# A retention layer with a feed-forward block: a fixed instruction order per engine in place of a software-pipelined loop

## Chip, cores, metric

One core of a Trainium2 chip. The metric is the time of one execution on the device in microseconds (us), the median of several runs. Engines are named as in the profile: PE (TensorE, matmuls), PEld (its weight loads), DVE (VectorE), ACT (ScalarE), POOL (GpSimd), SP (a queue that issues DMA transfers).

## The reference

Batch 4, 8 heads, 768 tokens, head size 64. First a retention recurrence per head; its output, with the heads side by side, is x (512 wide). Then a normalised feed-forward block with a residual:

```python
for t in range(S):
    state = gamma * state + einsum('bhd,bhe->bhde', k[t], v[t])
    y[t] = scale * einsum('bhd,bhde->bhe', q[t], state)
# x = y with the heads joined: [4, 768, 512]
xn = (x - mu) / sqrt(var + 1e-6) * g_ln
out = x + relu(xn @ w_ch1) @ w_ch2          # 512 -> 2048 -> 512
```

Both kernels work on tiles of 128 tokens: 24 tiles, 6 per batch entry, the recurrence in its chunked form (within a tile a masked 128x128 product, across tiles a state). Four tiles form a group, because the first product takes 512 tokens at once.

## The kernel before

One loop runs over the tiles. Each iteration has the work of several tiles in different stages: the first product runs six tiles behind the attention, the second nine behind. All inputs come as bf16 (converted in flight) on one DMA queue, which POOL issues, and one chunk of the weights follows each tile's q, k, v.

```python
for t in range(-2, NT + MM2_LAG):
    ...load_q(t+2); load_k(t+2); load_v(t+2)        # gpsimd queue, fp32 -> bf16
    ...vg = vsb * ks                                # DVE, later POOL
    # a quarter of the first product, tile t-6: four times
        for ko in range(KO): nc.tensor.matmul(pm1, w1[...], xnt[...])      # 512 wide
        nc.scalar.activation(out=h1[:, ho, :], in_=pm1, func=AF.Relu)
    # q and k of tile t+1 transposed into ptr (the one bank of tag "tp")
    # pa: 4 matmuls of one row half, then 4 of the other; two masks on DVE
    # second product of tile t-9: 16 matmuls, then the add and the store
    pxt = ptp.tile([P, H, P], BF16, tag="tp")       # xn of tile t-2, same bank as ptr
    for ko in range(KO): nc.tensor.transpose(pxt[:, ko, :], ...)
    for ko in range(KO): nc.scalar.mul(out=xnt[...], in_=pxt[:, ko, :], mul=gln[...])
    # py, pd of tile t-1
    nc.scalar.copy(out=x_all[:, ty, :], in_=py)     # ACT reads py
    ...ptmp = pd + pb_prev                          # DVE
    ...pb = ptmp * g128m                            # POOL
    nc.vector.bn_stats(out=stats, in_=py)           # DVE reads the same bank
    ...rstd, negms
    nc.scalar.activation(out=xn, in_=xg, func=AF.Identity, bias=negms, scale=rstd)
    # one chunk of w1 or w2 on the gpsimd queue
```

## Time and profile before

| | before |
|---|---|
| time, median of 3 runs (range) | 254.82 us (254.81 to 255.43) |
| span of the profiled run, PE busy | 253.1 us, 88% |
| first feed-forward product starts | 43.8 us (one matmul; the next at 44.6, which the prediction takes as the start) |
| one steady iteration | 9.06 us |
| last matmul ends | 249.0 us |

PE bounds this kernel once it has started, so its idle time is the table to read; the busy shares of the other engines (41 to 53%) bound nothing. The prediction below shows those lines. Two more come from the view of the waits (engine and line, what it waited for; microseconds in total, times, longest):

```profile
PE ptr L233 <- DMA qsb<-in_q_dram: 12.0, 7, 5.0
...
DVE stats L360 <- ACT x_all L334: 8.1, 18, 1.2
```

The first is the start, held up by q. The second looks harmless and was: DVE, which has plenty of idle time here, waits for ACT's copy before it may read the same PSUM bank.

### The profile page before, as it was taken

To read this page: it belongs to the slowest core of one execution; us is meant where nothing else is said; L and a number is where in the kernel's file an instruction comes from. 1 tells how busy PE (TensorE), PEld (TensorE's weight loads), DVE (VectorE), ACT (ScalarE), POOL (GpSimd) and SP (SyncE) were. 2 spreads that over 40 slices of the span, in tenths; PEclk is the share of its full clock that TensorE was granted. 3 is DMA by queue.
4 is the path that set the end of the run, shared out by engine and by line. 5 is a ranking of instruction groups with operands and counts; after the bars stand their busy time and mean duration, and the time that the engine had idled before them with its cause. 6 is when DMAs were issued, how large, how long until landed. Compare 5 with 4: busy or idle time off the path is not lost.

```text
span 253.1 us, 4043 instructions
## 1 busy us (share of the span) xinstructions
PE 222.4 (88%) x1577; PEld 118.0 (47%) x1600; DVE 104.5 (41%) x249; ACT 133.2 (53%) x295; POOL 109.7 (43%) x121
## 2 busy tenths in 40 slices
PE   0534666999999999999999999999999999999993
PEld 0323444555555545545554554555455444444441
DVE  5454476256364353535435434543544231111121
ACT  5133456699484476558447546744754475333100
POOL 8948589789985373337357530330110100000000
PEclk9999999999999999999999999999999999999999
DMA  6999999999999976494998550410110011111012
GB/s 42 119 182 183 186 176 175 172 88 108 95 125 105 62 85 80 65 65 62 93 68 91 71 40 39 62 44 0 44 41 19 25 43 41 41 44 41 12 71 83
DMA packets 83106, 20.18 MB, mean 80 GB/s; under 512 B 75920, under 2 KB 80016, under 8 KB 83088
## 3 DMA queue, kind: packets, MB, share of 16 engines
q0 software_dynamic: 79104, 13.64, 69.4%
q1 hardware_dynamic: 3984, 6.30, 6.6%
q8 instruction: 12, 0.20, 0.3%
q14 instruction: 6, 0.05, 0.0%
HBM read 27.27 MB, written 6.29 MB: 133 GB/s over the span
## 4 chain that ended last, share of the span: by engine, by line
PE 65%; ACT 14%; DMA 8%; DVE 5%; POOL 5%; issue 2%; POOLq 0%
PE pm L275 33%; PE pm L219 21%; DMA qsb<-in_q_dram 8%; ACT xntg L298 6%; DVE stats L360 3%; ACT h1g L226 3%; PE pa L250 2%; ACT x_all L334 2%; PE pxt L296 2%; PE ptr L233 2%; PE ptr L235 2%; ACT rstd L364 1%; POOL ksb L90 1%; POOL vsb L96 1%; ACT trs L240 1%
## 5 line engine op out<-in xcount | busy, mean ns | idle before, releaser
L219 PE MATMUL pm<-xntg,w 128*128 128x512 bf16 x364 | 88.6, 382 | 3.8 <-ACT h1g L226 1.6
L275 PE MATMUL pm<-w,h1g 128*128 128x512 bf16 x381 | 86.3, 380 | 0.2
L226 ACT ACTIVATE h1g<-pm 128x512 bf16<-128x512 f32 x96 | 55.5, 592 | 18.8 <-PE pm L219 14.6
L219 PEld LDWEIGHTS <-w 128*128 128x128 bf16 x384 | 36.7, 98 | 46.7 <-issue 9.9
L275 PEld LDWEIGHTS <-h1g 128*128 128x128 bf16 x384 | 36.3, 98 | 43.3
L298 ACT ACTIVATE xntg<-pxt,gln 128x128 bf16<-128x128 bf16 x96 | 27.4, 368 | 55.0 <-PE pxt L296 54.9
L283 DVE TENSOR_TENSOR osb<-pm,x_all 128x512 f32<-128x512 f32 x24 | 16.6, 692 | 76.9 <-PE pm L275 76.9
L257 DVE TENSOR_TENSOR asb<-pa,cm 128x512 bf16<-128x512 f32 x48 | 30.9, 683 | 7.7 <-PE pa L250 7.6
L203 POOL TENSOR_TENSOR vg<-vsb,ks 128x512 bf16<-128x512 bf16 x17 | 19.7, 1158 | 28.8 <-PE pd L342 19.2
L90 POOL DMA_DIRECT2D ksb<-in_k_dram x24 | 21.7, 906 | 20.2 <-PE pd L342 19.8
L355 POOL TENSOR_TENSOR pb<-ptmp,g128m 128x512 bf16<-128x512 bf16 x16 | 18.6, 1161 | 27.1 <-DVE ptmp L354 27.0
L237 DVE TENSOR_TENSOR trs<-ptr,qsT 128x512 bf16<-128x512 bf16 x24 | 10.2, 424 | 35.5 <-PE ptr L235 35.4
L84 POOL DMA_DIRECT2D qsb<-in_q_dram x24 | 21.9, 913 | 5.3 <-PE pa L250 2.2
L96 POOL DMA_DIRECT2D vsb<-in_v_dram x24 | 21.9, 916 | 3.6 <-POOL vg L203 1.8
L233 PE MATMUL ptr<-idn,qsb 128*128 128x128 bf16 x96 | 11.0, 245 | 12.0 <-DMA qsb<-in_q_dram 12.0
L376 ACT ACTIVATE xn<-x_all,negms,rstd 128x512 bf16<-128x512 bf16 x24 | 19.5, 811 | 3.1 <-DVE negms L367 2.4
L360 DVE BATCH_NORM_STATS2 stats<-py 128x6 f32<-128x512 f32 x24 | 16.7, 697 | 8.1 <-ACT x_all L334 8.1
L334 ACT CAST x_all<-py 128x512 bf16<-128x512 f32 x24 | 14.3, 597 | 9.4 <-PE py L326 5.7
L240 ACT COPY trs<-ptr 128x512 bf16<-128x512 bf16 x24 | 14.0, 585 | 6.5 <-DVE trs L237 6.5
L233 PEld LDWEIGHTS <-qsb 128*128 128x128 bf16 x96 | 7.6, 107 | 17.3 <-DMA qsb<-in_q_dram 13.3
L296 PE MATMUL pxt<-idn,xn 128*128 128x128 bf16 x96 | 10.1, 233 | 3.8 <-ACT trs L240 3.7
L250 PE MATMUL pa<-trs 64*128 64x128 bf16 x192 | 12.0, 243 | 1.6 <-ACT trs L240 1.6
(42 smaller groups left out, 137.1 us busy)
## 6 DMA issues: line engine op xcount, KB each, us to landing
out_dram<-osb SPq DMA_DIRECT2D x24, 256.0 KB, 2.0
w<-in_moe_w_ch_dram POOLq DMA_DIRECT2D x8, 512.0 KB, 9.0
qsb<-in_q_dram POOLq DMA_DIRECT2D x24, 128.0 KB, 4.5
ksb<-in_k_dram POOLq DMA_DIRECT2D x24, 128.0 KB, 4.4
vsb<-in_v_dram POOLq DMA_DIRECT2D x24, 128.0 KB, 4.2
gln<-in_moe_g_ln_dram SPq DMA_DIRECT2D x1, 2.0 KB, 2.2
```

The lines of the kernel that those rows point to most:

```text
L84: nc.gpsimd.dma_start(out=qsb, in_=qv[bl][cl])
L90: nc.gpsimd.dma_start(out=ksb, in_=kv[bl][cl])
L96: nc.gpsimd.dma_start(out=vsb, in_=vv[bl][cl])
L203: veng.tensor_tensor(out=vg, in0=vsb_of[ts_], in1=ks, op=ALU.mult)
L219: nc.tensor.matmul(pm1, lhsT=w1[:, ko, ho * P:(ho + 1) * P], rhs=xnt1[:, ko, :, :], start=(ko == 0), stop=(ko == KO - 1),)
L226: nc.scalar.activation(out=h1[:, ho, :], in_=pm1, func=AF.Relu)
L233: nc.tensor.transpose(ptr[:, pr, :], qsb[:, 2 * pr:2 * pr + 2, :], idn)
L257: nc.vector.tensor_tensor(out=asb[:, par_i], in0=pa, in1=cm4, op=ALU.mult,)
L275: nc.tensor.matmul(pm2, lhsT=h1[:, ho, q2 * P:(q2 + 1) * P], rhs=w2[:, ho, :], start=(ho == 0), stop=(ho == HO - 1),)
L298: nc.scalar.mul(out=xnt_of[tg][:, ko, ti, :], in_=pxt[:, ko, :], mul=gln[:, ko:ko + 1],)
L360: nc.vector.bn_stats(out=stats, in_=py.rearrange("p h d -> p (h d)"))
L376: nc.scalar.activation(out=xn, in_=xg, func=AF.Identity, bias=negms, scale=rstd)
```

## The change

The intent: start the dense part earlier (q and v take a second queue as fp32, weights are loaded between the token tiles), take work off ACT, DVE and POOL (g_ln goes into w1 once, the state is summed in PSUM), and write every engine's order by hand in place of a generic pipeline. The kernel declares its schedule manual: each engine's instructions keep the order in which they are written. The second product runs two groups behind the first. The core of the diff, with cuts:

```diff
-        qsb = qstg.tile([P, H, D], BF16, ...);  nc.gpsimd.dma_start(out=qsb, ...)
+        qsb[t] = qstg.tile([P, H, D], FP32, ...); nc.sync.dma_start(out=qsb[t], ...)
-    for t in range(-2, NT + MM2_LAG):
-        ... (above)
+    ctx.enter_context(tc.manual_schedule())
+    def scale_w1(j):                       # g_ln into a quarter of w1
+        for ko in range(KO):
+            nc.vector.tensor_scalar_mul(out=w1[:, ko, j*DM:(j+1)*DM], in0=..., scalar1=gln[:, ko:ko+1])
+    def att1(t, eng):   # ptr (tag "tp"): k and scaled q transposed; one copy of 1024 on ACT
+    def att2(t):        # pa: row halves in turn; one mask of 1024 on DVE
+    def att3(t):
+        # state part and tile part into py
+        nc.scalar.copy(out=x_all[:, t, :], in_=py)
+        nc.vector.bn_stats(out=stats, in_=py)
+        ...bn_aggr; sqrt on ACT
+        # pd: kept in PSUM, the next tile's matmuls add to it; pb = pd * mask on DVE
+        nc.vector.reciprocal(...)
+        nc.vector.tensor_scalar(out=xn[t], in0=x_all[:, t, :], scalar1=mv[:, 0:1], scalar2=rstd,
+                                op0=ALU.subtract, op1=ALU.mult)
+    def att4(t):        # pxt (tag "tp"): xn transposed; one copy of 512 on ACT
+    for t in range(GT):                    # the first four tiles, one after the other
+        scale_q(t, nc.gpsimd) ... scale_v(t, nc.vector)
+        att1(t); att4(t - 2) if t >= 2; att2(t); att3(t)
+    next_load(); next_load(); scale_w1(0)
+    att4(2); mm1(0, 0..1, tiles 0 to 2); att4(3); mm1(0, 0..1, tile 3)
+    def slot(a, g, quarter, m2, skip=0):
+        next_load()
+        scale_q(a, nc.gpsimd); scale_v(a, nc.gpsimd); att1(a)
+        # two chunks of the first product
+        if m2 is None and a - 1 in xn: att4(a - 1)
+        att2(a)
+        # two chunks of the first product
+        att3(a)
+        if m2 is not None:
+            mm2(m2)
+            att4(a)
+    for i in range(GT):
+        slot(4 + i, 0, i, None, skip=2 if i == 0 else 0)
+        if i < 3: scale_w1(i + 1)
+    att4(7)
+    for i in range(GT): slot(8 + i, 1, i, None)
+    att4(11)
+    for g in range(2, NG):                 # second product two groups later
+        for i in range(GT): slot(4*(g+1)+i or None, g, i, GT*(g-2)+i)
+    for t in range(GT*(NG-2), NT): mm2(t, tail=True)
```

## The prediction

> **What bounds the kernel now.** I read the page first: busy shares, then the slices.
>
> ```profile
> PE 222.4 (88%) x1577; PEld 118.0 (47%) x1600; DVE 104.5 (41%) x249; ACT 133.2 (53%) x295; POOL 109.7 (43%) x121
> ...
> PE   0534666999999999999999999999999999999993
> ...
> GB/s 42 119 182 183 186 176 175 172 88 108 95 125 105 62 85 80 65 65 62 93 68 91 71 40 39 62 44 0 44 41 19 25 43 41 41 44 41 12 71 83
> ```
>
> The row of PE has two parts. From the eighth slice on (44 us) TensorE is busy to the end; before that it works about half the time, and in just those slices the DMA engines move a level 180 GB/s. So there are two questions: how soon can the dense part start, and how much idle time is left in it. The chain of waits, in order of time, answers the first:
>
> ```profile
> 13.01 11.80 DMA qsb<-in_q_dram
> ...
> 32.48 7.60 DMA qsb<-in_q_dram
> ...
> 44.60 2.13 PE pm L219 x6
> ```
>
> The attention of the first seven tiles waits for q, which queues behind weights on the same full DMA queue. A tile of q, k, v and one weight chunk (0.92 MB as bf16) takes 0.92/180 = 5.1 us, and the first product (L219) starts only after seven such periods. For the second question I read TensorE's timeline over one steady iteration and near the end:
>
> ```profile
> 82.09 1.02 PE L219 MATMUL pm<-xntg,w 128*128 128x512 bf16 x4 [0.20 <-ACT h1g L226]
> 82.95 0.39 PE L233 MATMUL ptr<-idn,qsb 128*128 128x128 bf16 x4
> 83.18 0.39 PE L235 MATMUL ptr<-idn,ksb 128*128 128x128 bf16 x4
> 83.50 0.41 PE L250 MATMUL pa<-trs 64*128 64x128 bf16 x8
> 83.84 3.63 PE L275 MATMUL pm<-w,h1g 128*128 128x512 bf16 x16
> 87.30 0.39 PE L296 MATMUL pxt<-idn,xn 128*128 128x128 bf16 x4
> 87.52 0.40 PE L316 MATMUL py<-vg,asb 128*128 128x64 bf16 x8
> 87.76 0.39 PE L326 MATMUL py<-pb,trs 128*128 128x128 bf16 x4
> 87.98 0.39 PE L342 MATMUL pd<-vg,ksb 128*128 128x128 bf16 x4
> ...
> 209.99 0.39 PE L296 MATMUL pxt<-idn,xn 128*128 128x128 bf16 x4
> ...
> 210.83 1.89 PE L219 MATMUL pm<-xntg,w 128*128 128x512 bf16 x8 [0.46 <-ACT xntg L298]
> ```
>
> Differences of the starts give issue times: 16 second-product matmuls 3.46 us (216 ns each), four 128-wide ones 0.22 to 0.23, eight pa 0.34, eight py 0.23. A tile thus costs 2 x 3.45 for the two products and 0.45+0.34+0.23+0.22+0.22+0.23 = 1.69 for attention, 8.6 us. The iteration (82.95 to 92.01 for the next one's start) is 9.06, so some 0.4 us of it is stall. In all: 44.6 us of start; then 165.6 us of products and 28.4 of the remaining 17.7 tiles' attention (1.5 off for first and last chunks of a batch); the last matmul ends at 249.0. 249.0-44.6-194.0 = 10.4 us of stalls in the dense part. 4.1 us follow for the last add and store.
>
> The last two lines show a wait I need below: after a transpose into PSUM, a reader of ACT's copy of it is held. From 209.99, 0.39 for the matmuls, some 0.45 for one 128-wide ACT copy and the semaphores.
>
> **What the Trainium skill says.** "TensorE: Matmul & The Clock Gate", part 1: an array without sustained work runs at half rate. The trace agrees in its durations (four pxt at 27.44 took 0.58 us, later 0.39), though the granted clock reads 1.00 throughout. "VectorE: DVE Perf Modes", the TRN2 errata: an fp32 tensor-tensor takes (N+151)/0.96 ns, so one mask of 1024 elements is an estimated 1.22 us; the trace's 512-wide ones (about 690 ns) agree. "ScalarE: Activation LUTs", what ACT_TABLE_LOAD costs: 0.833 ns an element; from the 585 ns of the 512-wide L240 I estimate 585+427 = 1.01 us for one copy of 1024. "SBUF — State Buffer", who interferes with whom: a single-source DVE operation in a two-port mode and GpSimd lock each other out. No row of before shows it; the change brings such operations (xn, g into w1) beside two GpSimd multiplies per tile.
>
> **The change, part by part.**
>
> *Start.* q and v go to the SP queue and weights behind the first tiles, so data stops being the limit: 4 tiles at 2.5 us (q, k, v alone moved 155 to 160 GB/s around 45 us: 0.39 MB in 2.5) are there after some 12 us. What limits instead is the written order: att1, att2, att3 of one tile, then the next. At half clock I add up one tile: transposes 1.0, ACT copy 1.0, pa 0.62 (as at 14.30), mask 1.22, py with state 0.85, pd 0.43, and four hand-overs at 0.05: 5.3 us, 5.8 with a pxt between. With the first q scaled and transposed at about 5.5 us, four tiles end near 26.5. DVE then makes xn of tile 3 (about 2 us) before it can scale w1, so the first product starts near 28.5. Eight narrow products at a half-clock, att4(3) and its copy bring the first slot to 33 us. Before, at 44.6, had 2.3 more tiles of attention done (3.9 us), after has 1.7 us of product done: a lead of 44.6-33-2.2 = 9.4 us.
>
> *Slots 4 to 11 (no second product).* TensorE has 0.45+1.72+0.23+0.34+1.72+0.67 = 5.1 us a slot, ACT 4 relus at 0.51 issue time, copies of 0.92, 0.5, 0.5, and 0.25 for the root: 4.2 us. POOL has two multiplies at 1.16 and two issues at 0.9: 4.1. All fit. But scale_w1(i+1) is written after slot i, so on DVE it stands behind stats 0.7, aggregate 0.2, pb 0.69, reciprocal 0.15, xn 0.3: 2.0 us after the slot ends, then four scalings at an estimated 0.25. The next slot's first product should start at 0.45 and be over at 1.3; it is over at about 3.3. That is 2.0 us in each of three slots: 6 us. The shortened first slot (one product instead of two between the copy and its use) costs about 1.0.
>
> *Slots 12 to 23.* att4(a) is the last of a slot and att1(a+1) the first of the next, and both use the one bank of tag tp. TensorE must wait until ACT has copied pxt: drain 0.17 past the issue, 0.585 copy, hand-overs, about 0.84 us. It happens 14 times: after tiles 7, 11, 12 to 22, and after 23, where the product itself reads the copy: 11.8 us. The other latencies hide: mask 1.22+0.3 under two products of 1.72, the xn chain (2.5) under 3.46.
>
> *Taken away.* Adds of the state (ptmp 0.69 on DVE, pb 1.16 on POOL), four xntg turned into one copy (1.14 to 0.585 on ACT), xn from ACT (0.81) to DVE: all off TensorE; they remove most of the 10.4 us of stalls, which are ACT's relus being late. pa now alternates the two row halves; if pairs overlap fully, 0.34 falls to 0.24, over 20 tiles 2 us. I count 1.
>
> *End.* mm2(15) and mm2(16) share pm2: one wait of 0.95 us for the add. Splitting the last add changes nothing visible.
>
> Sum of differences against before: -9.4 (start) -10.4 (old stalls) +6 (w1) +1 +11.8 (tp) +0.95 -1 (pa) = -1.0 us, and some 1 to 2 us for DVE and POOL in each other's way: about 254 to 255 us.
>
> **Rivals.** (a) The fixed order does what it is meant to: hand-overs are shorter than I add, att4's copy and the w1 scaling cost half: 9 us less, some 246; a start at 25 instead of 28.5 would make it 242. For it: such details as the warmed root and the split last store look like an order worked out against measurements; against it: each wait above follows from written order and one buffer. (b) DMA still binds the first 30 us: 256-byte rows on the SP queue run slower than the POOL queue does, or keep k and w1 waiting. For it: the saturated 180 GB/s; against it: only half of the data is needed by then. It would cost 5 to 8 us: 258 to 262. (c) In the first eight slots POOL becomes the bound: 4.1 us of 5.1 by my count, but fp32 inputs may be slower than the bf16 rows of L203 (1.148 us). At 1.7 us a multiply it would match the slot; cost up to 3 us.
>
> **Range and chances.** My own sum is 254.5. I know two large waits that are exact in kind, and some small gains which I can't size, and a change of such detail is more often a gain than not; so I put the middle at 251, lower than the sum. The range 243 to 259 takes in (a) in part and (b) in part. The border of 2% is 249.7: faster 0.38, same 0.52, slower 0.10.
>
> **What would show it.** In the changed profile: first L-line of the first product near 28 us, slots from 33; three TensorE idles of about 2 us before the first product of a slot, released by the DVE scaling of w1; 14 idles of 0.6 to 0.7 us (past the drained pxt) before ptr, released by ACT xntg; slots with a second product of about 9.4 us; TensorE busy until about 249. I am wrong if the first product starts before 25 us or after 36, if idle before ptr is under 0.3 us, or if TensorE waits for a DMA after 35 us.

## The result, and the profile after

After takes 285.19 us (284.71 to 286.02); before, in the same rounds, 254.92 (254.81 to 255.43). The ratio is 1.119, with a 95% interval of 1.116 to 1.123: slower by 12%. Here and below a ratio is the mean time of one kernel's fast runs over that of the other's fast runs in the same rounds, so not quite the ratio of the medians quoted.

The page of after (busy lines; then 40 slices of the span, PE's busy tenths, its granted clock in tenths, and what the DMA engines moved):

```profile
PE 226.8 (80%) x1579; PEld 117.7 (42%) x1608; DVE 110.7 (39%) x201; ACT 114.8 (40%) x199; POOL 75.1 (26%) x83
...
PE   0455575486598749889889898988898899989994
PEclk9999997977989997999999999999999999999998
...
GB/s 148 231 206 196 194 193 210 169 196 187 103 11 25 31 20 2 95 53 113 129 58 93 129 105 37 82 113 37 25 17 37 37 39 37 37 39 74 74 74 74
```

As planned, ACT and POOL have less to do. PE's busy time is up by 4.4 us, though: the same products at a lower clock, as the four slices of 7 in PEclk suggest. And PE, which before had a row of nines from the eighth slice on, has eights in nearly every second slice. The DMA engines deliver 150 to 230 GB/s through the first ten slices and almost nothing in the five after the eleventh: from there the data is ahead of the work, not behind it.

By stages, from the starts of tiles 4, 8 and 12 (their first transposes) in the trace; the predicted column is worked out from the prediction's own terms (28.5 and 33 stated; then four slots of 5.1, the first one product shorter but 1.0 longer, with 6 of w1 waits and one tp wait of 0.84; four of 5.1 and one tp wait of 0.84; the last is what remains up to the 249.0 that it gave):

| stage | predicted | after | difference |
|---|---|---|---|
| up to tile 4's start (first product at 28.5 / 32.85) | 33 | 37.13 | +4.1 |
| tiles 4 to 7 | 26.5 | 39.65 | +13.1 |
| tiles 8 to 11 | 21.2 | 29.90 | +8.7 |
| tile 12 to the last matmul's end | 168.2 | 172.94 | +4.7 |
| last matmul ends | 249.0 | 279.62 | +30.6 |

Against before it is the same story: by 76.8 us before had issued 107 weight loads for the two products and the attention scores of 11 tiles, after only 72 (16 of them narrow ones that do the work of 8) and of 8 tiles. The lead of the start was gone before the second product had begun.

The stage of tiles 4 to 7, one hand-over from the timeline (start, duration, engine, line, operation, count, and the idle time before it with what ended it):

```profile
41.07 0.58 ACT L205 CAST x_all<-py 128x512 bf16<-128x512 f32 x1 [0.17 <-PE py L200]
...
41.69 0.70 DVE L207 BATCH_NORM_STATS2 stats<-py 128x6 f32<-128x512 f32 x1 [1.12 <-ACT x_all L205]
...
42.52 0.66 DVE L226 TENSOR_TENSOR pb<-pd,bm 128x512 bf16<-128x512 f32 x1
...
43.28 0.92 DVE L231 TENSOR_SCALAR xn<-x_all,mv,rstd 128x512 bf16<-128x512 bf16 x1
...
44.12 1.98 DVE L126 TENSOR_SCALAR w<-w,gln 128x512 bf16<-128x512 bf16 x4
...
45.37 2.95 PE L255 MATMUL pm<-xntg,w 128*128 128x512 bf16 x8 [3.67 <-DVE w L126]
```

Read downwards: DVE's statistics start only when ACT's copy of the same bank is over; then aggregate, pb, reciprocal, xn; then four scalings; then PE may go on, after 3.67 us. This happens in three slots, each time 3.67. And when PE does go on, its eight 512-wide products take 2.95 us here, 3.18 and 3.41 in the next two slots, and not the 1.89 of a warm array. The windows of after over this stage (length, then busy time and count of PE, PEld, DVE, ACT, POOL; the granted clock; DMA share; GB/s) show why:

```profile
36.00:48.00 12.00, 7.17 (x64) 3.94 (x64) 5.57 (x10) 5.62 (x11) 5.33 (x6) 0.93 1.39 203
48.00:60.00 12.00, 8.25 (x60) 4.26 (x59) 4.95 (x9) 5.37 (x10) 3.75 (x4) 0.78 1.17 177
60.00:72.00 12.00, 8.22 (x55) 4.11 (x56) 6.54 (x11) 5.09 (x10) 3.76 (x4) 0.86 1.25 195
```

The granted clock falls to 0.78. From the first product of one slot to that of the next are 10.57 us (45.37, 55.94, 66.51); the prediction had 5.1 + 2.0.

The steady stage, one seam between two slots with a second product:

```profile
134.01 1.05 POOL L141 TENSOR_TENSOR qg<-qsb,qsc 128x512 bf16<-128x512 f32 x1
...
134.81 1.41 DVE L231 TENSOR_SCALAR xn<-x_all,mv,rstd 128x512 bf16<-128x512 bf16 x1
135.02 1.04 POOL L149 TENSOR_TENSOR vg<-vsb,vsc 128x512 bf16<-128x512 f32 x1
...
136.28 0.40 PE L245 MATMUL pxt<-idn,xn 128*128 128x128 bf16 x4
...
137.35 0.38 PE L157 MATMUL ptr<-idn,ksb 128*128 128x128 bf16 x4 [0.67 <-ACT xntg L246]
```

The last line is the wait I predicted: ptr into the bank of pxt, held until ACT has copied it. The slot is 9.77 us long (127.58 to 137.35). The xn on DVE takes 1.41 us, ending right after POOL's second multiply; the same instruction takes 0.41 where POOL's multiplies are over or not yet begun. In the view of the waits of after:

```profile
POOL ksb L107 <- PE pd L217: 40.9, 6, 9.4
DVE stats L207 <- ACT x_all L205: 39.4, 24, 2.0
...
PE ptr L157 <- ACT xntg L246: 8.8, 13, 0.7
```

The first row returns in e5. The 39.4 us of the second are idle time of DVE, for most of which py is not there yet; the copy itself holds the statistics up by about 0.6 us each time (at 133.22, py was done at about 132.6).

### The profile page after: what moved, and what is told of

It reads as the page before. It is cut to its first block, busy times and chain, and to the rows that moved or that the text cites. A ratio compares the mean times of both kernels' runs of the same rounds, so it can differ in the third digit from the quotient of the medians.

```text
span 283.6 us, 3960 instructions
## 1 busy us (share of the span) xinstructions
PE 226.8 (80%) x1579; PEld 117.7 (42%) x1608; DVE 110.7 (39%) x201; ACT 114.8 (40%) x199; POOL 75.1 (26%) x83
## 3 DMA queue, kind: packets, MB, share of 16 engines
q0 software_dynamic: 29184, 7.34, 26.5%
## 4 chain that ended last, share of the span: by engine, by line
PE 65%; DVE 18%; ACT 11%; issue 3%; DMA 2%; DVEq 0%; ACTq 0%; POOLq 0%
PE pm L255 30%; PE pm L271 18%; DVE xn L231 5%; PE pm2b L271 5%; DVE stats L207 4%; PE pa L172 3%; ACT xntg L246 3%; ACT x_all L205 3%; PE pxt L245 3%; ACT h1g L262 3%; DVE pb L226 2%; DVE asb L180 2%; PE ptr L157 2%; DMA ksb<-in_k_dram 2%; ACT trs L163 2%
## 5 line engine op out<-in xcount | busy, mean ns | idle before, releaser
L255 PE MATMUL pm<-xntg,w 128*128 128x512 bf16 (+2 forms) x373 | 97.7, 400 | 16.1 <-DVE w L126 13.8
L262 ACT ACTIVATE h1g<-pm 128x512 bf16<-128x512 f32 (+2 forms) x98 | 57.3, 589 | 55.9 <-PE pm L255 53.1
L271 PE MATMUL pm<-w,h1g 128*128 128x512 bf16 x312 | 71.3, 379 | 1.1 <-DVE osb L284 0.8
L180 DVE TENSOR_TENSOR asb<-pa,cm 128x1024 bf16<-128x1024 f32 x24 | 29.4, 1224 | 67.6 <-PE pa L172 67.6
L107 POOL DMA_DIRECT2D ksb<-in_k_dram x24 | 22.2, 926 | 47.4 <-PE pd L217 40.9
L141 POOL TENSOR_TENSOR qg<-qsb,qsc 128x512 bf16<-128x512 f32 x24 | 25.3, 1054 | 32.0 <-DMA qsb<-in_q_dram 28.9
L207 DVE BATCH_NORM_STATS2 stats<-py 128x6 f32<-128x512 f32 x24 | 16.8, 699 | 39.4 <-ACT x_all L205 39.4
L149 POOL TENSOR_TENSOR vg<-vsb,vsc 128x512 bf16<-128x512 f32 x20 | 21.4, 1068 | 36.8 <-issue 20.5
L163 ACT COPY trs<-ptr 128x1024 bf16<-128x1024 bf16 x24 | 24.1, 1004 | 13.0 <-PE ptr L159 13.0
L246 ACT COPY xntg<-pxt 128x512 bf16<-128x512 bf16 x24 | 14.0, 584 | 29.4 <-PE pxt L245 29.4
L231 DVE TENSOR_SCALAR xn<-x_all,mv,rstd 128x512 bf16<-128x512 bf16 x24 | 18.9, 787 | 0.9
L205 ACT CAST x_all<-py 128x512 bf16<-128x512 f32 x24 | 13.9, 581 | 9.8 <-PE py L200 9.8
L271 PE MATMUL pm2b<-w,h1g 128*128 128x512 bf16 x62 | 14.4, 379 | 0.1
```

Source lines behind the costliest of these rows:

```text
L141: eng.tensor_tensor(out=qg[t], in0=qsb.pop(t), in1=qsc[:, c, :].unsqueeze(2).to_broadcast([P, H, D]), op=ALU.mult,)
L163: nc.scalar.copy(out=trs[t], in_=ptr)
L180: nc.vector.tensor_tensor(out=asb[t].rearrange("p a i t -> p (a i) t"), in0=pa.rearrange("p a i t -> p (a i) t"), in1=cm.unsqueeze(1).to_b ...
L205: nc.scalar.copy(out=x_all[:, t, :].rearrange("p (h d) -> p h d", d=D), in_=py)
L207: nc.vector.bn_stats(out=stats, in_=py.rearrange("p h d -> p (h d)"))
L231: nc.vector.tensor_scalar(out=xn[t], in0=x_all[:, t, :], scalar1=mv[:, 0:1], scalar2=rstd, op0=ALU.subtract, op1=ALU.mult,)
```

## The experiments

My theory after the result: (T1) the scaling of w1 behind the xn chain costs 3.67 us in each of three slots; (T2) such idles drop the clock, which costs about as much again; (T3) the single bank of tag tp costs 0.84 us a seam; (T4) DVE's xn and POOL's multiplies lock each other out. Rivals: (T5) reading py on two engines in turn is what delays it all; (T6) the start is bound by data, or its fp32 form; (T7) the second product two groups later leaves slots too short to hide the chain. All twelve kernels gave correct results. In all edits, after is the base. The measured times, to which the sections below refer. The medians are of all four runs; e3, e5, e7 and e10 have one slow run each, and their fast runs alone have medians of 280.60, 280.82, 288.15 and 255.81. The gains below are differences of the medians of fast runs, and good to 1 or 2 us by these intervals:

| run | us, median (range) | ratio to before | 95% |
|---|---|---|---|
| after | 285.19 (284.71 to 286.02) | 1.119 | 1.116 to 1.123 |
| e1_w1_early | 271.28 (269.66 to 273.64) | 1.063 | 1.057 to 1.070 |
| e2_xn_from_psum | 285.77 (283.05 to 286.85) | 1.118 | 1.111 to 1.125 |
| e3_stats_first | 280.88 (278.44 to 284.24) | 1.097 | 1.091 to 1.104 |
| e4_att4_late | 276.17 (275.43 to 277.58) | 1.083 | 1.078 to 1.087 |
| e5_deep_bufs | 280.95 (277.80 to 282.14) | 1.098 | 1.091 to 1.106 |
| e6_mm2_one_later | 280.81 (279.80 to 280.98) | 1.101 | 1.097 to 1.105 |
| e7_qv_bf16 | 289.02 (287.37 to 292.90) | 1.132 | 1.126 to 1.138 |
| e9_fill | 281.94 (280.79 to 282.29) | 1.107 | 1.103 to 1.112 |
| e10_two_groups | 256.96 (254.85 to 261.05) | 1.007 | 1.000 to 1.014 |
| e12_no_deep | 252.62 (251.09 to 254.24) | 0.993 | 0.987 to 0.999 |
| e8_first_sum | 251.26 (250.24 to 252.32) | 0.987 | 0.982 to 0.993 |
| e11_first_tiles | 251.02 (249.71 to 251.32) | 0.985 | 0.982 to 0.989 |

### e1_w1_early: the scaling of w1 ahead of the xn chain

```diff
-        slot(4 + i, 0, i, None, skip=2 if i == 0 else 0)
-        if i < 3: scale_w1(i + 1)
+        slot(..., sw=i + 1 if i < 3 else None)     # in slot, after att2(a): scale_w1(sw)
```

> One edit: the scaling of the next quarter of w1 is written after att2 of the running slot instead of after the slot. Theory A (order): the three idles of 3.67 us before a slot's first product are there because the scaling stands behind xn on DVE, and the half clock of slots 0 to 3 follows from those idles; then all three go, the first eight products of slots 1 to 3 take about 1.75 instead of 2.95 to 3.4 us, and the time falls by 3 x 3.7 + 3 x 1.4 = 15 us, less 3 to 5 us because the wait for xn before pxt shows instead: 270 to 275. Rival D (data): w1 arrives late and the idle stays under another name (a wait for the DMA): 283 to 285.

It gained 13.9 us. The timeline of this run, at the same place:

```profile
43.48 0.39 PE L159 MATMUL ptr<-idn,qg 128*128 128x128 bf16 x4
43.70 1.89 PE L255 MATMUL pm<-xntg,w 128*128 128x512 bf16 x8
```

No idle before the first product, 1.89 us for eight, and 6.1 us from one slot's first product to the next in place of 10.57. Tiles 4 to 7 take 26.9 us in place of 39.65. That stage had been lost to four DVE instructions in the wrong place, and to what PE's idling did to its clock. How much of it is the clock, e9 says.

### e9_fill: the same wait, but PE kept busy in it

Sixteen matmuls whose result nobody reads, ahead of the first product in each of the three slots. PE waits for DVE as before, but not idle; the kernel does 48 matmuls more.

```diff
+        if g == 0 and quarter > 0:
+            for _ in range(4):
+                pmd = pmm1p.tile([P, GT * P], FP32, name="pmd", tag="pm1")
+                for ko in range(KO): nc.tensor.matmul(pmd, lhsT=w1[:, ko, 0:P], rhs=xnt[0][:, ko, 0:GT, :], ...)
```

> The changed kernel with 16 idle-filling products (same operands, result not read) put into each of slots 1 to 3, where TensorE otherwise waits 3.67 us for the scaled w1. Theory C: part of the loss there is not the wait but the half clock that follows it (eight products take 2.95 to 3.4 us, not 1.75). Then the filled kernel, with 48 matmuls more, is faster: the granted clock stays at 1.0 between 37 and 77 us, the eight products take 1.75, and the time falls by 3 to 5 us, to 280 to 282. Rival: the slow eight products are paced by the scaling on DVE (0.5 us for each of four column blocks): no change, 285, or more by what the fill exceeds the wait.

With more work it is faster by 3.2 us, and the intervals of the ratios don't touch. Its timeline, then one of its windows:

```profile
42.70 3.62 PE L373 MATMUL pmd<-xntg,w 128*128 128x512 bf16 x15
...
46.54 2.04 PE L255 MATMUL pm<-xntg,w 128*128 128x512 bf16 x8 [0.23 <-DVE w L126]
```

```profile
48.00:60.00 12.00, 11.72 (x93) 6.00 (x93) 6.19 (x10) 6.56 (x12) 3.77 (x4) 1.00 1.28 189
```

The window that had a clock of 0.78 has 1.00, the eight products take 2.04 us, and the slots follow each other in 9.01 us (46.54, 55.55, 64.57) in place of 10.57. So the lost clock is 1.56 us a slot (tiles 4 to 7: 35.4 us for 39.65), and T2 is shown, if smaller than I had thought: the wait itself is the larger part. The 10.57 now adds up: 5.1 as predicted, 3.67 of wait, 1.56 of clock, 0.24 left over.

### e2_xn_from_psum and e3_stats_first: who delays xn

e2 lets DVE read xn's input from PSUM and no longer from SBUF; e3 lets the statistics read py before ACT's copy does.

```diff
-            out=xn[t], in0=x_all[:, t, :], ...
+            out=xn[t], in0=py.rearrange("p h d -> p (h d)"), ...
```

> One edit: xn reads py in PSUM (fp32) instead of x_all in SBUF[...]. Theory L (lock): xn takes 0.41 us alone and up to 1.75 beside GpSimd multiplies because they lock each other out; then every xn takes about 0.66 us whatever GpSimd does, pxt waits about 1 us less in slots 8 to 16, and the time falls by 5 to 9 us: 276 to 280. Rival: the long xn are late for another reason (semaphores, a write port that any DVE output needs): they stay between 0.6 and 1.8 and the time stays at 284 to 286.

```diff
-        nc.scalar.copy(out=x_all[...], in_=py)
         stats = mstat.tile(...)
         nc.vector.bn_stats(out=stats, in_=py)
+        nc.scalar.copy(out=x_all[...], in_=py)
```

> One edit: the statistics of py on DVE are written ahead of ACT's copy of py. Theory S: the two readers of the py bank run one after the other, and in after the statistics stand behind the copy, which stands behind the last relu on ACT (39 us of DVE waits in the waits' list); with the order turned the statistics start within 0.1 us of py and xn is done 0.6 to 1.1 us sooner. In eleven slots where pxt or the w1 scaling waits for xn that makes 6 to 10 us: 275 to 279. Rival: ACT's copy, now behind the statistics, holds the root and the next copy of ptr by as much, and the time is within 2 us of 285.

e2: no gain (285.8). But its page shows xn with one duration (busy total, then mean ns, over 24 instructions):

```profile
L231 DVE TENSOR_SCALAR xn<-py,mv,rstd 128x512 bf16<-128x512 f32 x24 | 19.4, 810 | 0.9
```

In the trace it is 0.81 at each of the 24, beside POOL or not; in after it is 0.41 to 1.75. So the slow xn of after comes from POOL: T4 holds as a mechanism. The slot fell from 9.77 to 9.53 us, which is 8.70 (e4's slot without a seam) + 0.84 to within 0.01. That 0.24 is what the lock costs a steady slot, and only in tiles 12 to 16 (0.58 in tile 15), 1.6 us in all: from tile 17 on, POOL's multiplies are over in time in after too, xn takes 0.41 and the slots are 9.53 or 9.30. It costs more in tiles 9 and 10, where xn takes 1.34 and 1.62 in after: PE's waits for it fall from 1.29 and 1.56 to 0.76 and 0.75. All this was given back elsewhere: tile 4 starts at 38.71 in this profile for 37.13 (k of tile 0 landed 0.5 later), and tiles 4 to 7 took 40.8 us for 39.65, where xn's 0.81 stands in front of the scaling as surely as the locked one did.

e3 gained 4.6 us: ACT now waits for the statistics, and not the reverse. In its one profile, which fell in a slow run and is a hint at most, xn starts earlier and meets more of POOL's multiplies (mean 1.05 us for 0.79). T5 is a part, of some 5 us, not the whole.

### e4_att4_late: the two users of the tp bank apart

```diff
-            if m2 is None and a - 1 in xn: att4(a - 1)
+            if a - 1 in xn: att4(a - 1)
...
             mm2(m2)
-            if a is not None: att4(a)
+            if a is not None and a % GT == GT - 1: att4(a)
```

> One edit: in the slots with a second product att4 of a tile is moved into the middle of the next slot (except for the last tile of a group). The prediction's step: one bank of tag tp costs 0.84 us at each seam of two slots; 9 of 14 seams go: 7.5 us, and where xn was later than the end of mm2 (tiles 12 to 16) another 0.5 to 1 us each: 275 to 278. Rival: the idle moves into the middle of the slot, where pxt must wait for the copy of ptr in the same bank: less than 3 us, 282 to 285.

It gained 9.0 us. The timeline of PE, from one slot into the next:

```profile
131.23 3.62 PE L271 MATMUL pm<-w,h1g 128*128 128x512 bf16 x16
134.69 0.39 PE L157 MATMUL ptr<-idn,ksb 128*128 128x128 bf16 x4
```

No idle, and a slot is 8.70 us (125.99 to 134.69), against the 8.6 of pure work that I had added up for before. Nine seams are gone (five remain, at the ends of groups). At 0.84 us each that makes 7.6 us; the waits for xn in tiles 12, 13, 14 and 16, 0.24 each, make another 1.0. T3 holds, with the size predicted.

### e5_deep_bufs: more buffers for k and scaled v

```diff
-kstg bufs=6, vgp bufs=3
+kstg bufs=8, vgp bufs=5
```

> One edit: kstg 6 to 8 and vgp 3 to 5 buffers, the GpSimd program unchanged. Theory L2: GpSimd's two multiplies fall on xn because GpSimd is blocked on a buffer that pd frees, so it starts just when the xn chain does; with deeper k and vg buffers it is qg, freed by ptr at the start of a slot, that holds GpSimd, its multiplies end under the products, and xn is 0.41 us in slots 8 to 16 where it was 1.2 to 1.75. In slots 12 to 16 that takes about 1 us of each, in slots 9 and 10 as much: 278 to 281. Rival: GpSimd meets another DVE operation or xn all the same, since it is blocked on something once a slot: within 2 us of 285.

It gained 4.4 us. The timeline of this run shows what the buffers move:

```profile
128.77 1.03 POOL L149 TENSOR_TENSOR vg<-vsb,vsc 128x512 bf16<-128x512 f32 x1
...
131.46 0.41 DVE L231 TENSOR_SCALAR xn<-x_all,mv,rstd 128x512 bf16<-128x512 bf16 x1
```

In after, POOL waits to load k until pd's matmuls free a buffer (the row of 40.9 us in the waits above), and so starts its multiplies just when DVE starts the xn chain: the same event releases both. With two buffers more, POOL goes when q lands, is done before, and xn takes 0.41. Against the profile of after, the stage from tile 12 on is 2.0 us shorter, that of tiles 8 to 11 1.2, and what lies before 1.2.

### e6_mm2_one_later: the second product one group later, not two

```diff
-    for i in range(GT): slot(8 + i, 1, i, None)
-    att4(11)
-    for g in range(2, NG):  ...  GT*(g-2)+i
+    for g in range(1, NG):  ...  GT*(g-1)+i        # w2 loaded earlier in the list of loads
```

> One part undone: the second product comes one group later instead of two (w2 loads moved ahead for it). Theory G: in slots 8 to 11 TensorE has only 5.2 us of work against an xn chain of 4 us that is needed within the next slot's first half, so they take 6 to 7 us; with a second product in them the chain is hidden as in the later slots, and the same work is taken off the tail: 8.4 us of stall becomes 4 x 0.85 or so, time 279 to 281. If the first slots' idles were all that matters (theory A alone), the time stays within 2 us of 285.

It gained 4.4 us. In after the slots of tiles 8 to 11 have one product to hide the chain under, and PE waits for xn there 1.29, 1.56 and 2.63 us. The timeline of after has the last of these, and the one of tile 7 ahead of it:

```profile
75.71 0.40 PE L245 MATMUL pxt<-idn,xn 128*128 128x128 bf16 x4 [2.53 <-DVE xn L231]
...
105.61 0.40 PE L245 MATMUL pxt<-idn,xn 128*128 128x128 bf16 x4 [2.63 <-DVE xn L231]
```

With the second product in them, the stage takes 40.9 us including four second products of 3.46, so 27.1 without, for 29.90. T7 is shown.

### e7_qv_bf16: q and v loaded as before

```diff
-        qsb[t] = qstg.tile([P, H, D], FP32, ...);  nc.sync.dma_start(...)
+        qsb[t] = qstg.tile([P, H, D], BF16, ...);  nc.gpsimd.dma_start(...)      # v alike
```

> One part undone: q and v are loaded as bf16 by the GpSimd queue again. Theory A (order, not data): k0 comes a little sooner, but GpSimd has 0.9 us more for each of two loads a tile and DVE is locked out more often; time 284 to 292. Rival D (the fp32 loads on the SP queue are what makes it slow, by holding k and w1 back): the first product starts before 30 us instead of 32.85 and the time falls by more than 4 us.

Slower by 3.0 us than after. T6 falls as a cause of the loss: the loads were the part of the change that did what it should. (The edit also gives POOL two more loads to issue for each tile, so the form of the data is not tested alone.) (This profile was a slow run; only the times are used.)

### e8_first_sum, e10_two_groups, e12_no_deep: the repairs together

e8 has the edits of e1, e3, e4, e5 and e6; e10 is e8 with the second product again two groups later; e12 is e8 with after's buffers.

```diff
+ e1 + e3 + e4 + e5 + e6      (e8)
- e6                          (e10)
- e5                          (e12)
```

Expected of e8:

> The edits of w1 early, statistics first, att4 late, deep buffers and second product one group later together. If the stalls are separate, their gains add: 14 (measured) + 9 (measured) + 4 (measured) + 5 + 5 = 37: 248 to 252, below the kernel before (255). If they share the same idle (for example because w1 early only uncovers the wait for xn that the others remove), less: 255 to 262.

Expected of e10:

> As e8_first_sum, but the second product two groups later, as in the change. If slots 8 to 11 without a second product still cost their share when the other stalls are gone (theory G), this is 3 to 6 us slower than e8: 254 to 257. If the xn chain, now shorter, fits into a short slot, it is within 1.5 us of e8 (251).

Expected of e12:

> As e8_first_sum, but with kstg 6 and vgp 3 as in the change. If the lock of GpSimd and DVE matters in the repaired order too, xn goes up to 1.3 to 1.9 us in most slots and the time is 2 to 5 us above e8: 253 to 256. If att4, moved to the middle of the next slot, has taken xn off the path, within 1.5 us of 251.

e8 takes 251.26 us, 1.3% less than before (clear of the noise, but under 2%). The single gains add to 13.9 + 4.6 + 9.0 + 4.4 + 4.4 = 36.3; together they give 33.9. So the loss is accounted for: five places in the written order and the buffers, nearly independent. One group later is worth 4.5 us also in company (e10). The buffers are worth 1.4 there, with intervals that overlap (e12), so perhaps nothing: once the statistics come first and only four slots end in att4, a slow xn is hidden. It takes 0.95 us on average in e12 and 0.60 in e8, and in each profile PE waits for it twice.

### e11_first_tiles: e8 with the first four tiles overlapped

```diff
     for t in range(GT):
         scale_q ... scale_v; att1(t)
+        if t >= 1: att3(t - 1, half=True)     # all but reciprocal and xn
         att4(t - 2) if t >= 2; att2(t)
-        att3(t)
+        if t >= 1: att3b(t - 1)               # reciprocal and xn
+    scale_w1(0)
+    att3(GT - 1)
```

> As e8_first_sum, with the first four tiles overlapped: the transposes of a tile stand ahead of py of the tile before, its mask ahead of xn of the tile before, and w1's first quarter is scaled ahead of the statistics of tile 3. The four tiles follow each other at 5.1 to 5.6 us in e8 because each chain of PE, ACT, PE, DVE, PE is finished before the next begins. Theory P: with the overlap a tile takes about 4.2, the first product starts near 26 instead of 30.5, and the time is 246 to 248. Rival: the tiles are held by the arrival of q and v, and the first product stays at 29 to 31: 250 to 251.5.

The first product starts at 26.83 us, 3.7 earlier than in e8, and 251.02 us come of it: no gain that the intervals show. The lead is lost tile by tile: tile 4 starts 3.8 us earlier than in e8, tile 5 3.4, tile 8 only 0.5 (60.21 for 60.69). POOL's scaling of v for one and the same tile, in the timeline of e8 and then of e11:

```profile
57.55 1.04 POOL L149 TENSOR_TENSOR vg<-vsb,vsc 128x512 bf16<-128x512 f32 x1 [4.72 <-DMA vsb<-in_v_dram]
```

```profile
57.07 1.04 POOL L149 TENSOR_TENSOR vg<-vsb,vsc 128x512 bf16<-128x512 f32 x1 [4.29 <-DMA vsb<-in_v_dram]
```

In both kernels POOL waits for v, up to 4.7 us at a tile, and v lands within 0.6 us of the same time however early the products begin: the two multiplies of v before it start at 40.30 and 48.45 in e8, 39.70 and 47.96 in e11. With the other waits repaired the loads (some 200 GB/s up to 50 us, w1 and w2 among them) are what these tiles run up against, and an earlier start only waits for them. (The granted clock reads 0.76 between 26 and 40 us and 1.00 in e8, but that does not set the two apart: the four transposes before tile 4 take 0.63 us in both.) The last 0.5 us and 1.1 more go in tile 8's slot, where the eight products run slow in e11 and not in e8; the timeline of e11, then of e8:

```profile
61.02 3.12 PE L263 MATMUL pm<-xntg,w 128*128 128x512 bf16 x8
```

```profile
61.13 1.89 PE L255 MATMUL pm<-xntg,w 128*128 128x512 bf16 x8
```

The waits for xn just before are 2.39 us in e11 and 2.12 in e8. From tile 9 on the two run in step, e11 1.1 us behind (the profile of e8 is of its fastest run). This is read from the traces, one execution of each; no run that moves the weights tests it.

## Why the prediction was wrong

I predicted 251.0 us with a range of 243 to 259 and gave "slower by over 2%" a chance of 0.10. It was 285.19.

**Step that failed: "Slots 4 to 11 (no second product)".** It said of scale_w1 "2.0 us after the slot ends" and "6 us" in all, and of ACT, PE and POOL "All fit". The kind was right (DVE's scaling releases PE, in three slots); the terms were wrong in three ways, and these two stages make 21.8 of the 30.6 us by which the last matmul came late.
- *The chain's length*: 3.67 us of wait for about 2.0, three times: 5.0 us more. I added durations as if the chain began when py was written. The statistics wait until ACT has copied the same bank (24 of 24 times in the waits), 0.6 us here. The Trainium skill says it: "PSUM — Partial Sum Buffer", Terms, counts two engines on one bank as a collision, "reads against reads included", so their reads have to take turns. The trace agrees: stats starts at 41.69, x_all ends at 41.65. I had the row for this in the profile of before, where it was hidden under a long slot, and did not carry it into a short one. The rest lies in xn at 0.92 for my 0.3, and in the first scaling of w1, beside POOL's qg, at 1.19 (the longest of the 16 in the trace) for my 0.25; these pieces overlap a little, so that they add to more than the 1.67.
- *The clock*: 1.56 us a slot, in three slots, that I put at nothing (e9). I had cited the page on the clock gate and gone on with full-speed durations, though I was adding idles of 2 us and more to a stage that had few matmuls.
- *The next four slots*: 5.1 us each predicted; 6.69, 5.89, 6.70 and 10.62 measured (from 76.78 to 106.68). The sums of busy time did "fit", but a chain through DVE and ACT from py to pxt has to fit as a latency, not as a share: three waits for xn make 5.5 us of the 8.7. A fourth, 2.53 us for the xn of tile 7, ends the stage before, and the eight products after it are slow again (3.38 us, from 77.35 to 80.73, for 1.72). Giving these slots the second product brings back 4.4 (e6).

**"Start"** was 4.3 us short: first product at 32.85, not 28.5. The view of the timeline of after, first and last:

```profile
6.78 0.61 PE L157 MATMUL ptr<-idn,ksb 128*128 128x128 bf16 x4 [6.78 <-DMA ksb<-in_k_dram]
...
32.85 2.74 PE L255 MATMUL pm<-xntg,w 128*128 128x384 bf16 x8 [2.75 <-DVE w L126]
```

k of tile 0 arrived at 6.78 us, where I had the first transposes done at 5.5 (my 2.5 us a tile was for bf16 loads, and q and v come as fp32, 0.66 MB a tile with k; but PE waits for no load after this one); the tiles then took 4.97, 5.91 and 5.90, close to the 5.3 to 5.8 predicted; from the last tile's end (29.47) to the first product 3.4 us passed, not 2, by the same chain as above.

**"Slots 12 to 23"** held: 0.84 us a seam as a sum, 0.67 past the drained pxt, all 14 times (13 before ptr, the last before the product itself), and a slot of 9.53 or 9.77 for "about 9.4". e4 gave 9.0 us for nine seams. Of the 4.7 us that this stage took longer, 1.6 are DVE and POOL in each other's way in tiles 12 to 16 (e2), which the prediction had put at 1 to 2 us in all; 1.4 more are the first slot, 11.13 us long, with slow products after the wait of 2.63; the rest is spread.

**"Taken away"** can be judged by e4's slot: 8.70 us for the 8.6 of pure work. The old stalls did go. The alternating row halves were worth nothing: eight pa matmuls take 0.33 us as before (0.34), where I counted 1 us in all.

**"End"** held: the view of the waits has one of 0.8 us before the second product for the add, where I had 0.95.

**Rivals.** (b), DMA as the bound, was wrong for after (e7; PE waits for a load once, for k of tile 0); it is what e11 ran into once the rest was repaired. (c), POOL as the bound, was wrong in its form: its fp32 multiplies take 1.05 us, less than the bf16 ones of before. What I lacked was the rival that came: POOL, off the critical path, released by the very event that releases DVE, and stretching an instruction that is on it from 0.41 to as much as 1.75 us.

**The choice of the middle.** My sum was 254.5 (its terms, -1.0 and then 1 to 2 on top of before, give 254.8 to 255.8); I moved it to 251 on the ground that such detail is more often a gain than not. The runs give no support for that; the sum itself was 30 us off, for its latencies, and a range of 16 us was too narrow for a rewrite in which three waits were added from durations alone.

## What to carry to other kernels

When an order is fixed by hand, follow each chain that ends in the bound engine as a latency, including the reads of one bank by two engines and whatever stands ahead on each engine's queue; busy shares that fit say nothing about a short slot. Work that is not urgent for its own tile but that PE waits for (here the scaling of w1) goes ahead of the long chain, not behind it. An idle of 3.67 us cost more than itself here, since the products after it ran at a lower clock (1.56 us more, e9). And a kernel that starts earlier than its data comes can end where it began (e11, as far as its traces show).

## What the Trainium skill lacked or had wrong

- "VectorE: DVE Perf Modes", the TRN2 errata: its row for reads from PSUM (120 + N cycles) makes an estimated 0.66 us of a tensor_scalar over 512 fp32 elements; it took 0.81 in 24 of 24 (e2). Its row for SBUF (58 + N/4) makes an estimated 0.19 us of the bf16 one; the uncontended xn took 0.41 and a scaling of w1 0.34. The page says itself that the fixed term is nearer 150 cycles (0.29 us); the form with two operations and two per-partition scalars (xn) took longer than the one with one of each (w1).
- "SBUF — State Buffer", who interferes with whom: the lock between DVE and GpSimd is confirmed (xn 0.41 alone, 1.41 beside two multiplies, flat 0.81 from PSUM). Not on the page: what two GpSimd instructions back to back do. DVE did not get through between them: xn began at 134.81, during the first (over at 135.06), and ended at 136.22, after the second (136.06), 1.0 us late; the latest was 1.34 late (1.75 for 0.41).
- "TensorE: Matmul & The Clock Gate", part 1: agrees that idling lowers the clock (0.78 over 12 us with idles of 3.67 us in it). Its ramp of under 1% is said of a typical kernel, and the page itself has a case that pays at every idle; here three idles cost 4.2 us of 285, 1.5% (e9). So nothing is wrong there, but the 1% is not to be carried over.
- "TensorEngine Tiling (Array Packing)", key properties: tiles are said to run in parallel. What an order of four and four costs against alternating ones no page says; alternating the halves brought nothing here (0.33 us for eight, for 0.34).
